# Keys and values as 5 tokens on 116 partitions, with full-width state products and a reordered prologue, in a linear-attention and SwiGLU kernel

## The chip, the cores and the metric

The kernel runs on one core of one Trainium2 chip. The metric is the device time in microseconds (us), the median of several executions. A profile covers one execution; its span is about 2 us shorter than that execution's device time. Engines are called by their short names: PE (TensorE matmul), PEld (its weight loads), DVE (VectorE), ACT (ScalarE), POOL (GpSimd) and SP (SyncE, which issues most transfers). The 16 DMA engines of the core carry all loads and stores.

## The reference, cut to what matters

```python
# q, k, v: (8 batches, 8 heads, 576 tokens, 64); weights 512 x 1536 (twice) and 1536 x 512, all float32
kv  = np.einsum('bhsd,bhse->bhde', k, v)          # a 64x64 state per head
out = np.einsum('bhsd,bhde->bhse', q, kv)
out = out / rms(out) * g_norm                     # per head
x   = out.transpose(0, 2, 1, 3).reshape(4608, 512)
xn  = x / rms(x) * rms_g
y   = (silu(xn @ w_gate) * (xn @ w_val)) @ w_out  # SwiGLU
```

## The kernel before

It rounds to bfloat16 and works batch by batch: 8 stages of 512 tokens, then a ninth with the 64 left-over tokens of all batches. While PE runs the feed-forward of one stage, the other engines prepare the attention of the next, and SP loads the batch after that. In this document "stage n" is the feed-forward of batch n, and the prologue is all work before stage 1: the loads of batches 0, 1 and 2, the weights, and stage 0.

Keys and values of a batch are each one load of 128 partitions with 9 tokens of one head per partition, so one run in DRAM is 9 x 64 x 4 = 2304 B. A pair of heads fills 128 partitions, and each head's state is formed in a 64x64 quarter of the PE array, by 72 small products per batch.

```python
def kv_view(src, b):
    return src[b].rearrange("h s d -> (h s d)").rearrange("(j p x) -> p j x", j=NS, p=128)

def load_kv(b, name, queue, js=slice(0, NS)):
    queue.dma_start(out=raws[b, name][:, js, :], in_=kv_view(srcs[name], b)[:, js, :])

def kv_pair(ps, b, j, first, last):
    for c in range(C):                                   # C = 9
        for u in range(2):
            rows = slice(u * D, u * D + D)
            PE.matmul(ps[rows, rows], lhsT=bufs[b]["k"][rows, j, c, :], rhs=bufs[b]["v"][rows, j, c, :],
                      start=(first and c == 0), stop=(last and c == C - 1))
...
for n in range(1, B + 1):                                # the stages
    ...
    steps[2].append(lambda n=n: load_batch(n + 2))       # q, k, v of batch n+2, all on SP's queue
    ...
    steps[0] += [lambda a=a: a.kv_products((0, 1))]      # state of batch n+1
    steps[11] += [... a.scale(0), a.x_rows(0) ...]       # rows for stage n+1, by DMA transpose on SP's queue
    steps[13].append(lambda b=b, c=c: atts[b].q_rows(c)) # q of batch n+2, by DMA transpose on SP's queue
```

Batch 2 is not ready when stage 1 starts, so stage 1 has a special order (`attend_late`). Three small loads come from POOL's queue.

## Time and profile before

| | before |
|---|---|
| device time, median | 337.96 us when the prediction was made; 336.3 to 337.6 in the later comparisons |
| span of the profile | 336.7 us |
| start of stage 1 | 64.9 us |
| stage 1, then a steady stage | 34.9 us, 33.6 us |
| loads of keys and values, alone on the DMA engines | about 390 GB/s |

The stage starts here and below are read from the timeline of PE: the first gate product (`g_ps`) after the down products of the stage before.

These lines are from the first page of the profile of the kernel before: PE's busy share in tenths, PE's granted clock in tenths, the mean busy share of the 16 DMA engines, and what they moved, in 40 slices of 8.4 us.

```profile
span 336.7 us, 5596 instructions
PE   5688999999899999999999999999999999999994
PEclk9999999999999999999999999999999999999998
DMA  8999996249058904790569056955400560050014
GB/s 257 344 378 390 372 367 235 95 102 375 24 140 182 335 3 125 172 357 5 133 169 354 2 138 155 275 217 138 113 0 0 140 111 0 3 167 20 2 31 93
```

For the first six slices the DMA engines are full at up to 390 GB/s: the prologue is bound by loads. Later PE is full and the DMA share swings between 0 and 9, with room to spare. The table of stretches (busy time and instruction count per engine, then clock, DMA share and GB/s) gives two numbers: one steady stage, and a piece of time in which only keys and values load.

```profile
100.05:133.60 33.55, 33.23 (x229) 16.09 (x232) 19.19 (x37) 20.14 (x35) 0.00 (x0) 1.00 0.56 154
80.00:84.00 4.00, 4.00 (x26) 2.00 (x25) 3.93 (x6) 2.73 (x6) 0.00 (x0) 1.00 1.05 392
```

A steady stage is PE's own time (33.23 of 33.55 us busy), and keys and values load at 392 GB/s with a DMA share of 1.05, that is on all 16 engines, about 24.5 GB/s each. The cost of the small state products shows in the timeline of PE (start, duration, then the instruction):

```profile
134.30 1.03 PE L427 MATMUL v_ps<-xnt,wv_sb 128*128 128x512 bf16 x4
135.26 0.76 PE L236 MATMUL att_ps<-vb,kb 64*64 64x64 bf16 x36
136.17 0.81 PE L427 MATMUL g_ps<-xnt,wg_sb 128*128 128x512 bf16 x3 [0.16 <-issue]
```

Four wide products take 0.86 us from start to start; here 1.87 us pass from 134.30 to 136.17, so this half of a batch's state costs about 1.0 us. By the next lines of the same view (a wide group at 136.82, the other half at 137.78, a wide group at 138.47) the other half costs 0.8 us.

### The profile page before, as it was taken

What the parts mean: (1) busy time and instruction counts of PE and PEld (TensorE: products, weight loads), DVE (VectorE), ACT (ScalarE), POOL (GpSimd) and SP (SyncE); (2) the same over time, 40 slices, a digit from 0 to 9 for tenths busy, and PEclk for the clock granted to TensorE, in tenths of its full rate; (3) what the DMA queues carried; (4) which work ended last, traced back from release to release, by engine and by line L of the source; (5) the groups of instructions that cost most, each with busy time, mean ns of one, the idle gap of its engine ahead of it and who ended that gap; (6) DMA issues with size and microseconds to landing.
All of it is one profiled execution on the core that took longest, in us unless ns stands there. A gap on an engine that the chain in (4) does not pass through costs nothing.

```text
span 336.7 us, 5596 instructions
## 1 busy us (share of the span) xinstructions
PE 317.4 (94%) x2157; PEld 157.3 (47%) x2195; DVE 180.3 (54%) x373; ACT 182.6 (54%) x319; POOL 14.3 (4%) x28
## 2 busy tenths in 40 slices
PE   5688999999899999999999999999999999999994
PEld 1466454555345444544454445444544444444441
DVE  5466643567913782378237824782478257823310
ACT  3476765766565556556645664566455245223321
POOL 6040230000000000000000000000000000000000
PEclk9999999999999999999999999999999999999998
DMA  8999996249058904790569056955400560050014
GB/s 257 344 378 390 372 367 235 95 102 375 24 140 182 335 3 125 172 357 5 133 169 354 2 138 155 275 217 138 113 0 0 140 111 0 3 167 20 2 31 93
DMA packets 61467, 54.89 MB, mean 163 GB/s; under 512 B 35837, under 2 KB 47105, under 8 KB 61441
## 3 DMA queue, kind: packets, MB, share of 16 engines
q1 hardware_dynamic: 61056, 53.95, 52.6%
q10 hardware_dynamic: 288, 0.59, 0.5%
q8 instruction: 17, 0.28, 0.4%
q14 instruction: 10, 0.07, 0.1%
q0 software_dynamic: 96, 0.00, 0.0%
HBM read 37.75 MB, written 9.44 MB: 140 GB/s over the span
## 4 chain that ended last, share of the span: by engine, by line
PE 86%; DVE 4%; DMA 4%; issue 2%; ACT 1%; SPq 0%; DVEq 0%
PE g_ps L427 26%; PE v_ps L427 26%; PE o_ps L440 25%; DMA st<-in_q_dram 3%; PE att_ps L236 3%; DVE h_sb L433 2%; PE att_ps L302 1%; DMA st<-in_k_dram 1%; PE g_ps L440 1%; PE v_ps L440 1%; PE att_ps L244 1%; DVE ssq L320 1%; PE att_ps L297 0%; DVE sq L319 0%; PE att_ps L372 0%
## 5 line engine op out<-in xcount | busy, mean ns | idle before, releaser
L433 DVE TENSOR_TENSOR h_sb<-silu,v_ps 128x512 bf16<-128x512 bf16 (+1 forms) x112 | 74.5, 666 | 116.9 <-PE v_ps L427 75.3
L427 PE MATMUL g_ps<-xnt,wg_sb 128*128 128x512 bf16 (+1 forms) x438 | 109.8, 371 | 2.4 <-issue 0.9
L427 PE MATMUL v_ps<-xnt,wv_sb 128*128 128x512 bf16 (+1 forms) x431 | 110.2, 371 | 1.4 <-DVE h_sb L433 0.5
L432 ACT ACTIVATE silu<-g_ps 128x512 bf16<-128x512 f32 (+1 forms) x112 | 65.5, 586 | 66.2 <-PE g_ps L427 65.6
L440 PE MATMUL o_ps<-wo_sb,h_sb 128*128 128x512 bf16 x399 | 89.7, 379 | 2.3 <-DVE h_sb L433 1.2
L427 PEld LDWEIGHTS <-wv_sb 128*128 128x128 bf16 x448 | 43.8, 98 | 50.1 <-issue 0.7
L440 PEld LDWEIGHTS <-h_sb 128*128 128x128 bf16 x432 | 42.1, 98 | 51.9 <-DVE h_sb L433 1.7
L427 PEld LDWEIGHTS <-wg_sb 128*128 128x128 bf16 x448 | 41.2, 98 | 42.3 <-issue 1.2
L104 ACT COPY o_sb<-o_ps 128x512 f32<-128x512 f32 x34 | 19.9, 587 | 44.8 <-PE o_ps L440 37.9
L320 DVE TENSOR_REDUCE ssq<-sq 128x16 f32<-128x1024 bf16 x28 | 34.2, 1220 | 1.0
L311 ACT ACTIVATE sq<-att_ps 128x512 bf16<-128x512 f32 x28 | 16.7, 597 | 14.4 <-PE att_ps L302 10.7
L104 ACT CAST vb<-st 128x576 bf16<-128x576 f32 x32 | 20.3, 671 | 3.9 <-DMA st<-in_v_dram 3.9
L334 DVE TENSOR_TENSOR xna<-outa,sy 128x512 bf16<-128x512 bf16 x28 | 17.5, 686 | 0.2
L236 PEld LDWEIGHTS <-kb 64*64 64x64 bf16 x576 | 11.3, 114 | 11.1 <-issue 6.0
L104 ACT CAST qb<-st 128x1024 bf16<-128x1024 f32 (+1 forms) x15 | 14.2, 984 | 4.0 <-DMA st<-in_q_dram 4.0
L313 ACT CAST outa<-att_ps 128x512 bf16<-128x512 f32 x28 | 16.2, 580 | 0.0
L236 PE MATMUL att_ps<-vb,kb 64*64 64x64 bf16 x576 | 13.1, 199 | 3.2 <-DVE kb L106 2.9
L104 ACT CAST kb<-st 128x576 bf16<-128x576 f32 x20 | 12.5, 674 | 0.0
L319 DVE TENSOR_TENSOR sq<-sq,gsq 128x512 bf16<-128x512 bf16 x28 | 11.7, 418 | 0.0
L302 PEld LDWEIGHTS <-qt 128*128 128x128 bf16 x96 | 7.4, 98 | 5.7
L302 PE MATMUL att_ps<-kv_all,qt 128*128 128x128 bf16 x96 | 9.3, 219 | 0.0
L515 PE MATMUL att_ps<-warm_sb 128*128 128x512 bf16 x12 | 6.3, 629 | 1.2 <-DVE warm_sb L470 1.2
(121 smaller groups left out, 132.7 us busy)
## 6 DMA issues: line engine op xcount, KB each, us to landing
out_dram<-o_sb SPq DMA_DIRECT2D x16, 512.0 KB, 3.1
st<-in_k_dram SPq DMA_DIRECT2D x7, 1152.0 KB, 9.8
st<-in_v_dram SPq DMA_DIRECT2D x7, 1152.0 KB, 12.1
st<-in_q_dram SPq DMA_DIRECT2D x7, 1024.0 KB, 7.2
st<-in_moe_w_out_dram SPq DMA_DIRECT2D x3, 1024.0 KB, 10.9
st<-in_moe_w_gate_dram SPq DMA_DIRECT2D x2, 1024.0 KB, 11.1
st<-in_moe_w_val_dram SPq DMA_DIRECT2D x2, 1024.0 KB, 12.5
st<-in_k_dram SPq DMA_DIRECT2D x4, 288.0 KB, 6.8
```

What stands on the lines that cost most here:

```text
L104: engine.copy(out=dst, in_=src)
L236: PE.matmul(ps[rows, rows], lhsT=bufs[b]["k"][rows, j, c, :], rhs=bufs[b]["v"][rows, j, c, :], start=(first and c == 0), stop=(last and c ...
L302: PE.matmul(cols, lhsT=self.qt[:, j, 128 * c : 128 * c + 128], rhs=kv_all[:, self.n, j, :], start=(j == 0), stop=(j == NS - 1),)
L311: SC.activation(out=self.sq[c][:, 0], in_=ps, func=ACT.Square)
L313: SC.copy(out=self.outa[c], in_=ps)
L319: DVE.tensor_tensor(out=sq[:, 1], in0=sq[:, 0], in1=gsq8, op=OP.mult)
L320: DVE.reduce_sum(out=self.ssq[:, c], in_=sq, axis=AX.X)
L334: DVE.tensor_tensor(out=self.xna[c], in0=self.outa[c], in1=self.alpha[:, c, :].to_broadcast([128, H, D]), op=OP.mult)
L427: PE.matmul(ps[:, 0:w], lhsT=wt[:, s, j * 128 : (j + 1) * 128], rhs=x[:, s, lo:hi], start=(s == 0), stop=(s == NS - 1),)
L432: SC.activation(out=silu[:, 0:w], in_=g_ps[:, 0:w], func=ACT.Silu)
L433: DVE.tensor_tensor(out=self.h[:, j, lo:hi], in0=silu[:, 0:w], in1=v_ps[:, 0:w], op=OP.mult)
L440: PE.matmul(self.o_ps[c], lhsT=self.h[:, j, c * 128 : (c + 1) * 128], rhs=wo_sb[:, j, :], start=(j == 0), stop=(j == NF - 1),)
```

## The change

The intent was to give PE fewer and fuller state products, to get batch 2 ready before stage 1, and to trim the prologue. Keys and values now lie with 5 tokens of every head on each of 116 partitions (115 x 5 + 1 = 576; the 116th partition holds one token). A pair of heads gives one 128-wide product per token slot, of which the two diagonal 64x64 blocks are kept: 20 products per batch for 72. The casts of batch 2 move to POOL ahead of stage 1, whose special order goes away. The first half units of stage 0 come two to a bank. The small loads leave POOL's queue. The core of the diff, cut:

```diff
-    C = 2 * S // 128
+    TK, PK = 5, 115
-    def kv_view(src, b):
-        return src[b].rearrange("h s d -> (h s d)").rearrange("(j p x) -> p j x", j=NS, p=128)
...
-    def load_kv(b, name, queue, js=slice(0, NS)):
-        queue.dma_start(out=raws[b, name][:, js, :], in_=kv_view(srcs[name], b)[:, js, :])
+    def load_kv(b, name, queue, hs=slice(0, H)):
+        src, dst = srcs[name], raws[b, name]
+        last = b == B - 1
+        for p0, n, t0 in ((0, PK, 0), (PK, 1, S - TK)) if last else ((0, PK + 1, 0),):
+            view = bass.AP(
+                tensor=src.tensor, offset=src.offset + ((b * H + hs.start) * S + t0) * D,
+                ap=[[TK * D, n], [S * D, hs.stop - hs.start], [1, TK * D]],
+            )
+            queue.dma_start(out=dst[p0 : p0 + n, hs, :], in_=view)
...
     def kv_pair(ps, b, j, first, last):
-        for c in range(C):
-            for u in range(2): ...                       # 18 products of 64x64
+        hs = slice(2 * j, 2 * j + 2)
+        longer = TK - 1 if b == B - 1 else 0
+        for t in range(TK):                              # 5 products of 128x128
+            n = PK + 1 if t == longer else PK
+            PE.matmul(ps, lhsT=bufs[b]["k"][0:n, t, hs, :], rhs=bufs[b]["v"][0:n, t, hs, :],
+                      start=(first and t == 0), stop=(last and t == TK - 1))
...
-    GP.dma_start(out=gam[0:NS, :], in_=moe_rms_g.rearrange("(s p) -> s p", p=128))
+    nc.scalar.dma_start(out=gam[0:NS, :], in_=moe_rms_g.rearrange("(s p) -> s p", p=128))
...
+    alloc_q(2)                                           # ahead of stage 1
+    for i in range(4):
+        cast_q(2, slice(2 * i, 2 * i + 2), GP)
+    for name in ("k", "v"):
+        for j in range(NS):
+            cast_kv(2, name, j, GP)
...
-        if n == 1:
-            attend_late(steps, 2, 0)
-            finish(steps, 2, 11)
-        elif n < B:
+        if n < B:
```

The last batch has its own pair of transfers, since the general view would read past the end of the tensor.

## The prediction

> **What bounds the kernel now.** PE: the chain of waits is 86% PE, and from 65 us on it is dense. In the table of stretches a steady batch takes 33.55 us with PE busy 33.2; the timeline shows four 128x512 matmuls per 0.86 us, so 144 are 31.1 us. The rest is 16 row products (0.9 us) and 72 small 64x64 state products (about 1.5 us). Batch 1's stage takes 34.96 us. Before 65 us DMA is the limit: from 4 to 55 us the DMA share is 1.02 to 1.14 at 320 to 390 GB/s, 24.3 GB/s per engine at 389 GB/s over 16; q0's last piece lands at 15.2 us, the first gate product runs at 23.8.
>
> **What the change should win.** State products: 20 full-width ones at 0.055 us (row products: 0.22 us per four) make 1.1 us for 1.5: 0.4 us in each of 7 batches, 3 us. Batch 1's stage becomes a normal one, 1.5 us. Fewer small evictions in the prologue: 2 to 4 us. With loads as fast as now I would say about 330 us.
>
> **What I think it costs.** The partition count. The Trainium skill, "DMA: Bandwidth & Descriptors", section "Why a DMA increments its semaphore by 16 and not by 1", says that a transfer runs on the largest k of at most 16 engines that divides the slowest dimension of both patterns. 128 partitions give 16; 116 = 4 x 29 gives 4; the last batch's 115 gives 5. No transfer of before tests this. If it holds, one key or value load (116 x 8 x 1280 B = 1.19 MB) puts 297 KB on each of four engines: 12.2 us at 24.3 GB/s (estimate) where 16 engines need 3. Everything queued behind it, weights and transposes too, waits for those four.
>
> *Prologue* (estimate, adding up the four engines' queue): batch 0's pieces and half of q land at about 28 us instead of 13, gate weights at 30 to 45, k1 57, v1 70, output weights 72 to 80, k2 95, v2 108. VectorE and ScalarE stall in order on the casts of k1 and v1, so batch 0 ends at about 90 us (65 now). Batch 2's state products then stop PE until about 110 us: some 42 us lost by there.
>
> *Steady batches*: DMA share 0.56 of 33.55 us is 18.8 us per engine, of which keys and values are 6.1. On engines 0 to 3 that becomes 18.8 - 6.1 + 24.4 = 37.1 us, above PE's 33.1. The four stages that load batches 3 to 6 stretch to about 37 us (+16 in all); later ones keep the gain.
>
> Sum: 338 + 42 + 16 - 8 = 388 us.
>
> **What would show each step.** Key and value loads of about 12 us each, at about 95 GB/s; the first gate product at 35 us or later; in the waits, k and v loads ahead of casts on VectorE, ScalarE and GpSimd; PE idle over 15 us ahead of batch 2's state products; steady stages near 37 us; 20 state products in about 1.1 us. If key and value loads still move over 300 GB/s, the step is wrong, and I expect 326 to 335 us.
>
> **What would make it wrong.** The division by 16 engines being done otherwise (13%); four engines alone running faster than 24.3 GB/s each; stalls hidden better by the reordered prologue, or worse.
>
> Predicted 388 us, 8 in 10 between 355 and 412; faster by over 2% 0.11, within 2% 0.04, slower by over 2% 0.85.

## The result, and the profile after

The changed kernel takes 424.93 us (median of 4, 422.12 to 428.53) against 337.63 us. Executions over 1.5% slower than the fastest of the same kernel are left out of the means. The ratio is 1.257 (95% interval 1.248 to 1.267). Here and below a ratio is the mean time of one kernel's fast runs over that of the other's of the same rounds, so it is not quite the ratio of the medians quoted.

The direction and the cause that were predicted came out, and the size did not: 388 us with a range of 355 to 412 was named. The same lines of the first page, now of the changed kernel (slices of 10.5 us):

```profile
span 420.3 us, 4813 instructions
PE   3426966199049999991999699979968999999995
PEclk9965896779659999997999799989997999999999
DMA  3269624962493297229627662789395006104004
GB/s 105 92 158 345 245 93 125 274 228 94 144 184 125 94 169 192 88 95 164 196 94 101 162 195 91 101 191 215 118 133 162 2 11 130 60 2 150 1 2 100
```

Many slices now stand at a DMA share of 2 to 3 tenths and 88 to 105 GB/s, where those of before stood at 9 tenths and over 340. PE has holes down to 0, and its clock dips after each. The table of stretches shows a piece of time with only keys and values loading, and two stages:

```profile
170.00:178.00 8.00, 8.00 (x43) 3.76 (x41) 6.32 (x10) 4.34 (x8) 0.00 (x0) 1.00 0.27 89
156.00:198.10 42.10, 33.31 (x180) 15.98 (x181) 19.19 (x37) 21.25 (x37) 0.00 (x0) 0.96 0.62 133
198.10:236.90 38.80, 34.84 (x180) 16.30 (x181) 19.20 (x37) 20.21 (x35) 0.00 (x0) 0.94 0.61 143
```

A DMA share of 0.27 is 4.3 of 16 engines, and 89 GB/s over four engines is 22 GB/s each. That is what four engines would look like. In the waits (who waited for whom, us in total, times, longest) the largest two are, as before, DVE and ACT waiting for PE. What is new below them are the transfers, and the casts that wait for them:

```profile
ACT vb L105 <- DMA st<-in_v_dram: 68.3, 10, 20.8
DVE kb L107 <- DMA st<-in_k_dram: 27.8, 5, 8.3
PE g_ps L434 <- DMA xnt<-xna: 22.3, 5, 8.8
PE att_ps L242 <- POOL vb L107: 15.7, 1, 15.7
```

On the first page of the kernel before, ACT's casts of v waited 3.9 us for their loads, for 68.3 here (instruction, then count, busy us, mean ns, idle us before it and who ended it):

```profile
L104 ACT CAST vb<-st 128x576 bf16<-128x576 f32 x32 | 20.3, 671 | 3.9 <-DMA st<-in_v_dram 3.9
```

The last line of the waits is PE standing still for 15.7 us in front of batch 2's state products, as predicted (over 15 us). `xnt<-xna` are the transposes that start a stage: they are issued on the same queue behind the loads. The timeline of SP in stage 3, which starts at 198.1 us, shows the order of one steady stage:

```profile
196.05 5.40 SPq L279 DMA_TRANSPOSE qt<-qb  x4
201.55 0.52 SPq L492 DMA_DIRECT2D out_dram<-o_sb  x1
202.17 0.39 SPq L137 DMA_DIRECT2D st<-in_q_dram  x1
202.61 0.97 SPq L127 DMA_DIRECT2D st<-in_k_dram  x1
203.63 10.99 SPq L127 DMA_DIRECT2D st<-in_v_dram  x1
226.09 8.53 SPq L350 DMA_TRANSPOSE xnt<-xna  x4
```

The transposed rows stand behind the loads: in the DMA records the last key or value packet of this stage ends at 234.2 us, and the next stage starts at 236.9.

### The profile page after: what moved, and what is told of

It is laid out like the page before. It is cut to its first block, busy times and chain, and to the rows that moved or that the text cites. A ratio compares the mean times of both kernels' runs of the same rounds, so it can differ in the third digit from the quotient of the medians.

```text
span 420.3 us, 4813 instructions
## 1 busy us (share of the span) xinstructions
PE 337.6 (80%) x1791; PEld 164.4 (39%) x1791; DVE 178.5 (42%) x364; ACT 178.8 (43%) x304; POOL 19.1 (5%) x39
## 4 chain that ended last, share of the span: by engine, by line
PE 60%; DMA 24%; SPq 9%; issue 3%; DVE 2%; POOL 1%; ACT 1%; POOLq 0%; ACTq 0%; DVEq 0%
PE g_ps L434 21%; PE v_ps L434 20%; PE o_ps L470 14%; DMA st<-in_v_dram 13%; DMA st<-in_k_dram 6%; SPq L350 5%; DMA xnt<-xna 4%; SPq L127 3%; PE att_ps L242 2%; PE att_ps L308 1%; DMA st<-in_moe_w_val_dram 1%; POOL kb L107 1%; DVE xna L343 1%; SPq L510 1%; DVE h_sb L440 0%
## 5 line engine op out<-in xcount | busy, mean ns | idle before, releaser
L440 DVE TENSOR_TENSOR h_sb<-silu,v_ps 128x512 bf16<-128x512 bf16 x104 | 71.1, 684 | 173.1 <-PE v_ps L434 159.2
L434 PE MATMUL g_ps<-xnt,wg_sb 128*128 128x512 bf16 x416 | 113.3, 397 | 31.8 <-DMA xnt<-xna 22.3
L434 PE MATMUL v_ps<-xnt,wv_sb 128*128 128x512 bf16 x416 | 113.9, 398 | 6.4 <-DVE h_sb L440 6.0
L439 ACT ACTIVATE silu<-g_ps 128x512 bf16<-128x512 f32 x104 | 62.6, 602 | 94.9 <-PE g_ps L434 94.8
L105 ACT CAST vb<-st 116x640 bf16<-116x640 f32 x28 | 19.3, 722 | 68.3 <-DMA st<-in_v_dram 68.3
L242 PE MATMUL att_ps<-vb,kb 115*128 115x128 bf16 (+1 forms) x160 | 15.3, 255 | 34.3 <-ACT vb L105 18.6
L242 PEld LDWEIGHTS <-kb 115*128 115x128 bf16 (+1 forms) x160 | 13.6, 118 | 41.2 <-issue 26.9
L343 DVE TENSOR_TENSOR xna<-outa,s1y 128x512 bf16<-128x512 bf16 x28 | 17.5, 687 | 0.2
L107 DVE CAST kb<-st 116x640 bf16<-116x640 f32 x8 | 4.4, 556 | 27.8 <-DMA st<-in_k_dram 27.8
L105 ACT CAST kb<-st 116x640 bf16<-116x640 f32 x20 | 13.5, 727 | 0.6 <-DMA st<-in_k_dram 0.6
L548 PE MATMUL att_ps<-kv_all 128*128 128x256 bf16 (+1 forms) x25 | 8.4, 490 | 1.2 <-DVE sel L534 1.2
```

Of the source, the lines that this page charges most:

```text
L105: engine.copy(out=dst, in_=src)
L242: PE.matmul(ps, lhsT=bufs[b]["k"][0:n, t, hs, :], rhs=bufs[b]["v"][0:n, t, hs, :], start=(first and t == 0), stop=(last and t == TK - 1),)
L343: DVE.tensor_tensor(out=self.xna[c], in0=self.outa[c], in1=self.alpha[:, c, :].to_broadcast([128, H, D]), op=OP.mult)
L434: PE.matmul(ps, lhsT=wt[:, s, j * 128 : (j + 1) * 128], rhs=x[:, s, :], start=(s == 0), stop=(s == NS - 1),)
L439: SC.activation(out=silu, in_=g_ps, func=ACT.Silu)
L440: DVE.tensor_tensor(out=self.h[:, j, :], in0=silu, in1=v_ps, op=OP.mult)
```

## The experiments

The theory: 116 partitions make a load run on 4 DMA engines, and this alone turns a small gain into the loss. The rivals: the new layout's packets of 1280 B for 2304 B; the new schedule; PE's clock. Twelve kernels ran, all with correct results. The table first; the sections below say what each was for. "Packet" is the median duration of one key or value packet in the trace's DMA records. A time is the median of all runs of a kernel.

| run | time, us | ratio to before | packet, ns |
|---|---|---|---|
| before | 336.3 to 337.6 | 1 | 95 (2304 B) |
| the change | 424.93 | 1.257 | 56 (1280 B) |
| change, 112 + 4 partitions | 343.06 | 1.017 | 91 |
| change, 114 + 2 | 375.05 | 1.109 | 55 |
| before, 124 + 4 | 442.48 | (see text) | 95 |
| change, idle products added | 420.43 | 1.247 | 56 |
| change, all 128 partitions | 332.67 | 0.990 | 60 |
| before, 112 + 16 | 343.27 | 1.020 | 156 |
| change, 128 in batches 0 to 2 | 372.71 | 1.104 | 56 |
| change, 128 from batch 3 on | 392.68 | 1.168 | 59 |
| change, q loaded earlier | 429.48 | 1.272 | 56 |
| change, 116 in batch 0 only | 353.61 | 1.051 | 60 |
| change, 116 in batch 2 only | 351.63 | 1.045 | 60 |
| before, 64 + 64 | 344.44 | 1.023 | 181 |

### Is it the number of engines? (112 + 4, and 114 + 2)

```diff
-        for p0, n, t0 in ((0, PK, 0), (PK, 1, S - TK)) if last else ((0, PK + 1, 0),):
+        one = ((0, PK, 0), (PK, 1, S - TK)) if last else ((0, PK + 1, 0),)
+        two = ((0, 112, 0), (112, 3, 112 * TK), (PK, 1, S - TK)) if last else ((0, 112, 0), (112, 4, 112 * TK))
+        for p0, n, t0 in two if True else one:        # or 114 and 2 in place of 112 and 4
```

> The changed kernel with one edit: each key or value load is two transfers, of partitions 0 to 111 and of the last 4 (in the last batch 112, 3 and 1). Tokens, partitions, packets of 1280 B, casts, products and schedule stay as they are. Theory (116 partitions put a load on 4 engines, 112 put it on 16): the two loads of a batch fall from 26 us to 7 or 8, TensorE's clock stays up, and the time is 326 to 333 us, below before. Rival A (the packets of 1280 B for 2304, or 116 used partitions, make the loads slow): still over 400 us. Rival B (the new schedule, with GpSimd's casts of batch 2 and the moved loads, costs a good part): 345 to 400 us.

> As the run with 112 and 4, but split into 114 and 2 partitions: 114 = 6 x 19 gives 6 engines by the rule. Theory: about 140 GB/s while keys and values load alone, 8.7 us for one load, 17 us for the two of a batch; the steady stages are then bound by TensorE again (about 33.1 us) and only the prologue pays: 350 to 370 us. Rival (any transfer of partitions that is not a multiple of 16 falls to one slow rate): near the 425 us of the changed kernel. Rival (only an extra transfer was needed): as the run with 112 and 4.

Cutting a load in two, with nothing else changed, took 82 us off (424.93 to 343.06). So neither the new schedule nor the layout is the main cause. With 114 + 2, where the rule gives 6 engines, the fast runs took 370.6 to 376.0 us (375.05 is the median with the slow run in it), just above the range expected. The stretch of time with only keys and values loading agrees with 6 engines: a share of 0.41 is 6.6 engines, 144 GB/s is 24 GB/s on each. This line is from the table of stretches of the profile with 114 + 2:

```profile
42.00:48.00 6.00, 5.89 (x12) 3.43 (x12) 1.93 (x5) 3.37 (x7) 2.69 (x4) 1.00 0.41 144
```

(The profiled execution of that kernel was an odd one, 1881 us with PE several times slower throughout; it is left out of the times, and stays unexplained. Only its loads are used.)

But 343.06 us misses the expectation of 326 to 333. The load rate says why. In the profile with 112 + 4, while only keys and values load:

```profile
34.00:39.00 5.00, 4.86 (x23) 1.97 (x21) 2.87 (x6) 4.01 (x7) 2.69 (x4) 1.00 1.11 228
```

The share is full, on 16 engines, yet they move 228 GB/s and not 392, and a packet takes 91 ns where the same packet takes 56 ns on four engines. So 16 engines alone are not the whole story.

### Does it need the new layout? (before with 124 + 4)

```diff
-        queue.dma_start(out=raws[b, name][:, js, :], in_=kv_view(srcs[name], b)[:, js, :])
+        for p0, p1 in ((0, 124), (124, 128)):
+            queue.dma_start(out=raws[b, name][p0:p1, js, :], in_=kv_view(srcs[name], b)[p0:p1, js, :])
```

> The kernel before with one edit: each key or value load is two transfers, of 124 and of 4 partitions; 124 = 4 x 31 gives 4 engines by the rule. Same bytes, same packets of 2304 B, nothing else of the change. Theory: a load takes about 12.2 us on four engines (297 KB at 24.3 GB/s), and the time is 395 to 425 us, as bad as the changed kernel or nearly. Rival (the slowness belongs to the new layout or the new schedule): within 2% of 338 us.

No: the old kernel with 124 = 4 x 31 partitions takes 442.48 us (434 to 448.5). Its runs scatter so much that no ratio is given; the fastest, 433.95 us, is 1.29 times the 336.68 of before. All four lie above the 395 to 425 us expected. Bytes, packets and schedule are those of before, and the loads run at 0.27 and 101 GB/s, as the table of stretches shows:

```profile
170.00:178.00 8.00, 7.95 (x44) 3.88 (x44) 6.32 (x10) 4.99 (x10) 0.00 (x0) 1.00 0.27 101
```

Why it is even slower than the changed kernel is open. In places (from 126 to 132 us and from 210 to 216 us of its trace) its loads fall to 60 to 70 GB/s: four engines are still busy, but one packet takes 148 to 178 ns there, near the 181 ns of the run with 64 + 64 below. No run asked why.

### Why are 112 partitions slow? (128 everywhere; before with 112 + 16 and with 64 + 64)

The changed layout can be loaded with all 128 partitions: partitions 116 to 127 receive tokens of the next head that nothing reads (a tenth more bytes).

```diff
+        fast = ((0, 112, 0), (112, 3, 112 * TK), (PK, 1, S - TK)) if last else ((0, 128, 0),)
+        for p0, n, t0 in fast:
```

> The changed kernel with each key or value load (but the last batch's) as one transfer over all 128 partitions; partitions 116 to 127 receive tokens of the next head that nothing reads. Packets stay 1280 B, bytes rise by a tenth. In the run with 112 and 4 partitions, packets took about 100 ns while keys and values loaded, against 56 ns on four engines, so 16 engines moved only about 215 GB/s. Theory (112 partitions are cut into 16 shares of 7[...]): packets near 56 ns, over 320 GB/s, the prologue 10 us or more shorter than there: 326 to 334 us. Rival (reads of 1280 B are slow on 16 engines whatever the partitions): 343 to 350 us.

> The kernel before with each key or value load in two transfers, of 112 and of 16 partitions; both counts give 16 engines. Packets stay 2304 B. Theory (shares of 7 partitions collide[...]): packets of 2304 B take 1.5 times or more the 95 ns of before, and the time rises by 8 to 16 us (346 to 354 us). Rival (the slow packets come with the 1280 B of the new layout): packets near 95 ns, within 1% of before.

> The kernel before with each key or value load in two transfers, of partitions 0 to 63 and 64 to 127. Both give 16 engines by the rule of divisors, and packets stay 2304 B. The Trainium skill (SBUF, the section on the DMA port swizzle) says that partitions 0 to 63 reach only 8 of the 16 ports. Theory (besides the number of engines, the ports that the partitions reach set the rate, which would explain the 156 ns packets of the run with 112 and 16): packets of 2304 B take 1.4 times or more the 95 ns of before, unless both halves run at once and share the ports out; the time rises by 4 to 10 us. Rival (only a share of 7 partitions, uneven to something else, was slow): packets near 95 ns, within 1% of before.

With 128 partitions the 1280 B packets take 60 ns, the loads run at 364 GB/s, and the kernel takes 332.67 us: ratio 0.990 (0.986 to 0.994), faster than before by about 1%. So packets of 1280 B are not slow on 16 engines. The reverse holds too: the 2304 B packets of the kernel before take 156 ns with 112 + 16, 1.5 times or more their 95 ns as expected. Its time, 343.27 us, rose by 6.9 us and so less than the 8 to 16 expected. With 64 + 64, a count that gives 16 engines as well, they take 181 ns, and the time rises by 7.5 us; both are in the expected ranges. The stretches with only keys and values loading, of 128, of 112 + 16 and of 64 + 64:

```profile
32.00:36.00 4.00, 4.00 (x20) 1.86 (x19) 1.22 (x2) 3.04 (x6) 2.69 (x4) 1.00 1.07 364
```

```profile
119.00:123.00 4.00, 4.00 (x24) 1.95 (x23) 3.49 (x6) 2.37 (x5) 0.00 (x0) 1.00 1.05 210
```

```profile
119.00:123.00 4.00, 3.95 (x23) 1.90 (x22) 2.83 (x4) 2.50 (x5) 0.00 (x0) 1.00 1.06 221
```

All three have every engine busy; the rate differs. The Trainium skill, "SBUF — State Buffer", section "Door 1: The DMA port swizzle", says that partitions 0 to 63 reach 8 of 16 ports of that memory, with an asymptote of about 218 GB/s. The 221 GB/s with 64 + 64 agrees; no record names the port. For 112 partitions, the theory of the first two of these runs, it is only an argument from that page's map: of 16 engines that each walk through 7 neighbouring partitions, some would stand on the same port while others are free. This is not shown, and a rival stays open: 112 + 4, 112 + 16 and 64 + 64 are all two transfers on 16 engines, and no run loaded 112 partitions in one.

### Where the loss falls: prologue and steady stages

The same edit, for batches 0 to 2 only, or from batch 3 on only.

> 128 partitions per load for batches 0 to 2, the changed kernel's 116 for batches 3 to 7. Theory: the prologue runs at full speed (batch 2's stage starts near 98 us as before or earlier), and the four stages that follow stay near 39 to 42 us: about 26 us above the run with 128 everywhere: 353 to 362 us.

> The reverse: 116 partitions for batches 0 to 2, 128 for batches 3 to 6 (the last in 112, 3 and 1). Theory: the prologue loses what it loses in the changed kernel (batch 2's stage starts near 156 us) and the steady stages fall to about 33.1 us: 55 to 65 us above the run with 128 everywhere: 384 to 398 us. The two losses add up to the whole within 5 us if they are independent.

The length of each stage, from the timelines (us). The profile of 128 in batches 0 to 2 is of a run that counts as slow (378.13 us; the fast runs took 369.0 to 374.0), so its stages are 4 to 9 us too long in sum:

| kernel | start of stage 1 | 1 | 2 | 3 | 4 | 5 | 6 |
|---|---|---|---|---|---|---|---|
| before | 64.9 | 34.9 | 33.6 | 33.6 | 33.6 | 33.6 | 33.6 |
| the change | 103.4 | 52.6 | 42.1 | 38.8 | 39.2 | 40.3 | 35.2 |
| 128 in batches 0 to 2 | 62.9 | 46.5 | 41.3 | 42.7 | 39.0 | 40.5 | 34.8 |
| 128 from batch 3 on | 102.2 | 53.2 | 34.0 | 33.1 | 33.1 | 33.1 | 33.1 |
| 128 everywhere | 62.8 | 33.1 | 33.8 | 33.1 | 33.1 | 33.1 | 33.1 |

With slow loads in the prologue only, the kernel takes 392.68 us: 60 us above the 332.67 of 128 everywhere, inside the expectation. With slow loads in the steady stages only it takes 372.71 us, 40 us above (38 to 39 by the fast runs alone), where 26 were expected. The expectation left out stage 1. It loads batch 3, and in the profile PE waits 13.0 us at its end for the transposed rows behind that load. In the changed kernel this load overlaps with the wait for batch 2. So the two losses overlap by 7 to 8 us (60 + 39 or 40 against 91 or 92). They are not independent within the 5 us that the expectation allowed.

### How much of a slow load is exposed in the prologue (batch 0 alone, batch 2 alone)

The edit is the same with the condition that the batch is not 0, or not 2.

> 128 partitions per load for all batches but batch 0, which has 116. Theory: each pair of prologue loads costs the difference between four engines and sixteen, about 26 - 6.5 = 19.5 us, fully exposed: first gate product near 41 us (21.0 with 128 everywhere), everything later shifted by as much: 350 to 355 us. Rival (my prediction's view, that the other prologue work hides a part): 342 to 348 us.

> 128 partitions per load for all batches but batch 2, which has 116. Theory: TensorE stops ahead of batch 2's state products, since that pair is last in the prologue's queue; before, they landed some 10 us or more ahead of their use, so here a part is hidden and 8 to 14 us are lost (341 to 347 us), fewer than the 19.5 us that the third pair adds in the changed kernel, where the queue was already late. Rival (fully exposed again): 350 to 355 us.

One slow pair of loads costs 353.61 - 332.67 = 20.9 us in batch 0, and 351.63 - 332.67 = 19.0 us in batch 2. In the DMA records batch 2's pair takes 29.3 us on four engines for 9.3 with 128 everywhere (the packets of other loads run in between), 20.0 us more, so nearly all of it is exposed. For batch 2 this went against my expectation: I had thought that its loads landed well ahead of their use. They don't. With 128 everywhere POOL waits for k and then casts k and v without a pause:

```profile
57.42 4.22 POOL L107 CAST kb<-st 116x640 bf16<-116x640 f32 x4 [1.24 <-DMA st<-in_k_dram]
61.59 2.71 POOL L107 CAST vb<-st 116x640 bf16<-116x640 f32 x4
```

The last packet of v ends at 60.5 us and the last cast at 64.3, 1.5 us after stage 1 starts, just as PE comes to the state products. With 116 in batch 2 only, PE stands there for 18.75 us:

```profile
81.72 1.36 PE L244 MATMUL att_ps<-vb,kb 116*128 116x128 bf16 x10 [18.75 <-POOL vb L107]
```

Batch 1 was not slowed alone. If its pair costs as much as the mean of the other two, three pairs make 60 us, which is what slow loads in the prologue alone cost.

### What sets a steady stage (q earlier), and the clock

```diff
-            steps[2].append(lambda n=n: load_batch(n + 2))
+            steps[2].append(lambda n=n: load_batch(n + 2, n > 1))     # keys and values alone, from batch 4 on
+        if n + 3 < B:
+            steps[12].append(lambda n=n: load_q(n + 3))
```

> The changed kernel, but from batch 4 on the load of q is issued in the stage before, behind the transposes of the normalised rows; keys and values are issued where they were. Same bytes. In the trace of the changed kernel a steady stage is a loop: about 6 us from its start to the issue of the loads, some 4 us for q, 26 us for keys and values on four engines, 3.4 us for the transposed rows that start the next stage: 39 us. Theory (the loop's sum sets the stage): stages 2 to 5 lose 2.5 to 4 us each, 9 to 15 us in all (410 to 416 us). Rival (the four engines' total work sets it, wherever q stands): within 3 us of the changed kernel.

The theory's 9 to 15 us did not come. Stages 2 to 5 became 40.4, 40.4, 40.5 and 39.3 us, no shorter on the whole (160.6 us for 160.4). The total is 4.5 us above the changed kernel, more than the rival's 3, but the intervals of the two ratios overlap (1.263 to 1.281 and 1.248 to 1.267). In the profile it is stage 1 that grew, from 52.6 to 60.5 us: its pair, that of batch 3, took 33.1 us in the DMA records for 26.3. The edit does not touch that pair, and why it was slow is open.

Nor does this run decide between theory and rival, for the edit hardly moved keys and values. The early q load now stands in front of the q transposes, and these stand in front of keys and values. By SP's timelines keys are issued 6.5 and 5.9 us after the start of stages 2 and 3, for 6.2 and 4.5 in the changed kernel. What both traces show is a sum of three parts. In stage 3 of the changed kernel the first key packet starts 9.7 us into the stage, the pair takes 26.4 us, and the next stage begins 2.7 us later: 38.8. With q earlier it is 8.9, 28.7 and 2.8: 40.4. Whether the order of issue or the work of the four engines sets the first part stays open.

```diff
+        if 2 <= n <= 5:      # after the down products
+            idle = att_pool.tile([128, 512], FP32, name="att_ps")
+            for _ in range(24):
+                PE.matmul(idle, lhsT=wg_sb[:, 0, 0:128], rhs=wo_sb[:, 0, :], start=True, stop=True, ...)
```

> The changed kernel plus 24 idle 128x512 products on TensorE (5.2 us at full clock) after the down products of batches 2 to 5, where TensorE waits for the transposed rows of the next batch. The trace of the changed kernel shows half clock at the start of these stages (four products in 1.7 us for 0.86). Theory: the clock stays up at the start of four stages, each saves 1 to 2 us: 4 to 8 us less than the changed kernel (416 to 421 us). Rival (the half clock hides behind the loads, which set the stage's length): within 2 us of it.

The timeline of the changed kernel shows the cold start of stage 3, with the wait in brackets:

```profile
198.12 1.86 PE L434 MATMUL g_ps<-xnt,wg_sb 128*128 128x512 bf16 x4 [8.78 <-DMA xnt<-xna]
```

These four products take twice their usual time. The Trainium skill, "TensorE: Matmul & The Clock Gate", Part 1, says that the clock falls to half after an idle window of about 3.4 us; this trace agrees, after 8.78 us of idleness. With the idle products the kernel takes 420.43 us, 4.5 us less and inside the expectation, but not for the reason given, and the size is not firm: the intervals of the two ratios overlap (1.242 to 1.253 and 1.248 to 1.267), and the two profiled executions differ by only 1.2 us. The products kept the clock up at the start of stages 4, 5 and 6 (four products in 0.86 us). In stage 3, 2.90 us of waiting were left after them, and the first four products still took 1.4 us. Stages 4 and 5, which did start at full clock, took 39.8 and 39.9 us for 39.2 and 40.3: no shorter, because the loads set their length. Stage 6, which loads nothing, went from 35.2 to 33.1 us. So the half clock is a consequence that costs about 2 us where nothing else hides it.

## Why the prediction was right or wrong, point by point

**Right: the mechanism.** A transfer's engines are the largest number up to 16 that divides its slowest dimension. The Trainium skill, "DMA: Bandwidth & Descriptors", section "Why a DMA increments its semaphore by 16 and not by 1", states the rule. This case agrees at 4 engines (116 and 124 partitions: share 0.27, 89 to 101 GB/s) and at 6 (114: share 0.41, 144 GB/s). Summed over a pair of loads in the DMA records, the packets keep 4.0 to 4.3 engines busy in the changed kernel, and 5.1 for its last batch (115 partitions, 5 by the rule, 111 GB/s). Undoing it in the changed kernel removes the whole loss, and doing it alone to the kernel before causes one at least as large.

**Right: the gain with fast loads, "about 330 us", range 326 to 335.** It is 332.67 us with 128 partitions, but luck is in it: 338 - 330 was a gain of 8 us, and 3.8 us were measured (336.42 for the kernel before), with a tenth more bytes to load. The state products do win what was said: PE's timeline of that kernel has

```profile
96.75 1.03 PE L436 MATMUL v_ps<-xnt,wv_sb 128*128 128x512 bf16 x4
97.62 0.73 PE L244 MATMUL att_ps<-vb,kb 116*128 116x128 bf16 x10
98.18 1.03 PE L436 MATMUL g_ps<-xnt,wg_sb 128*128 128x512 bf16 x4
```

From 97.62 to 98.18 is 0.56 us for half a batch, 1.1 us for 20 products as predicted, and a steady stage is 33.1 us for 33.6, the 0.4 us predicted. (The 72 small products cost 1.8 us by the timeline above and not 1.5; where the difference went is not known.) Stage 1 is 33.1 us for 34.9, and the prologue 2.1 us shorter.

**Wrong: the size. 388 us was the sum 338 + 42 + 16 - 8; three of its terms were off.**

1. *"some 42 us lost by there"* (the prologue). Slow loads in the prologue alone cost 60 us over the same kernel with fast ones. Two things were off. The queue was too short: at 12.2 us a load I had v of batch 2 land at 108 us and its products run at 110. Its last packet ends at 119.7 us in the DMA records, and the products ran at 121.0 (batch 0 ended at 103.4, for 90). And a loss of 42 us sets these 110 us against some 68, as if the new order had about 10 us to spare between load and products. It has not: with 128 everywhere the products run at 64.5 us, and a slow pair costs 19 to 21 us (batches 0 and 2, above). The step also took the transfers to run strictly one after another. The table of stretches of the changed kernel shows that they do not:

```profile
60.00:70.00 10.00, 4.02 (x11) 1.46 (x10) 3.83 (x7) 0.60 (x1) 0.00 (x0) 0.74 0.27 94
70.00:80.00 10.00, 3.23 (x12) 1.17 (x10) 0.00 (x0) 0.00 (x0) 0.00 (x0) 0.84 0.96 210
```

From about 72 us the output weights start on all engines, while v of batch 1 is still loading and lands only at about 81 us (predicted: 70): in the DMA records its packets then take about 111 ns for 56.

2. *"The four stages that load batches 3 to 6 stretch to about 37 us (+16 in all)"*. Slow loads from batch 3 on add 424.93 - 392.68 = 32 us to a kernel whose prologue is slow already. Stages 2 to 4 are 42.1, 38.8 and 39.2 us, not 37.1. The mis-sized term is the 24.4 us for keys and values on four engines: I had taken 24.3 GB/s per engine, from other packets. In this trace a packet of 1280 B takes 56 ns, which is 22.9 GB/s, where 2304 B in 95 ns are 24.3. The pair takes 26.4 to 27.8 us in stages 2 to 4. With 26.4 (stage 3) and the rest of the sum, 18.8 - 6.1 = 12.7 us, a stage would be 39.1 us, near the 38.8 measured. I had also written that "later ones keep the gain", but stage 5, which loads batch 7 on 5 engines, took 40.3: there the q rows of the ninth stage, in runs of 256 B, load first and keep all engines busy for about 5.5 us in the DMA records, so that the pair starts 16.3 us into the stage. Stage 2 is 3.3 us longer than stage 3 because its pair starts later (11.1 us into the stage for 9.7), takes longer (27.8 us for 26.4) and is followed by a longer rest (3.2 us for 2.7); what lies behind these is open.

3. *"- 8"*. Even with fast loads the gain was 3.8 us. In the changed kernel there is no room for it. The state products, the new stage 1 and the trimmed prologue all save time of PE, DVE or ACT, and I subtracted it from stretches that I had just said are bound by loads. Only stages 6 to 8 are bound by PE, and of these only stage 6 has state products, with a cold start of 2 us on top.

The three together are the missing 37 us, to within 1: 56 us (392.68 against 336.4) where 42 - 8 = 34 stood, and 32 us where 16 stood, are 88 us for the predicted 50.

**Right: the signs.** Loads of 13 to 15 us (12 predicted; pairs of 26.3 to 30.0 us), the first gate product at 41.7 us ("35 or later"), the waits for k and v on DVE, ACT and POOL, and PE's 15.7 us in front of batch 2's state products all showed up.

## What to carry to other kernels

Before changing a layout, factor the partition count of every load it produces: 116 partitions were fuller for PE than 64 and cost 92 us against the same kernel with 128, because 116 = 4 x 29. A count that gives 16 engines can still be slow (112 with a small second transfer, at 210 to 228 GB/s), so load 128 partitions, with rows that nobody reads if need be: that version, at 332.67 us, beats both kernels. And when a change makes one resource the limit, do not subtract savings of another in the same stretch.

## What the Trainium skill lacked or had wrong

- "DMA: Bandwidth & Descriptors": the rule for the number of engines held. The page asks for "ideally the 128 partitions", but states no rate for another count that gives 16 engines. Here 112 partitions with a second transfer of 16 or 4 move 210 GB/s (2304 B packets, 156 ns for 95) and 228 GB/s (1280 B packets, 91 ns for 60), where 128 move 392 and 364.
- The same page gives no measured duration of a packet at these sizes. Medians here are 56 ns for 1280 B (on four engines), 88 ns for 2048 B (weights) and 95 ns for 2304 B.
- "SBUF — State Buffer": nothing wrong was seen. The rate with 64 + 64 partitions, 221 GB/s, is near the asymptote stated for 64, about 218. That two halves in two transfers don't add up holds here too: before with 64 + 64 is 2.3% slower than with 128.
- "TensorE: Matmul & The Clock Gate": 2.90 us of waiting were once enough for half the clock (stage 3 of the run with idle products; the ends of products are modelled), a little under the window stated. That a cold start costs nothing where a load sets the stage (stages 4 and 5 took 79.7 us together with the clock up, 79.5 without) was found on no page.
